# Last 128 tokens of the second product stored in column pieces, on two queues

## The chip, the core and the metric

The kernel runs on one core of a Trainium2 chip. The time is that of the whole program on the device, in microseconds (us), as the median of several runs. A profile comes from one further execution; its span runs from the first to the last instruction that the profiler records.

## What is computed

The reference is an attention layer followed by a two-layer perceptron. Shapes: q, k and v are 8 batches x 12 heads x 448 positions x 64; w_in is 768 x 2048, w_out 2048 x 768; the output has 3584 tokens (8 x 448) of 768 float32 values.

```
scores = scale * np.matmul(q, k.transpose(0, 1, 3, 2))
attn = softmax(scores)
x = np.matmul(attn, v)  ->  (B * S, H * D)
h = x @ w_in
g = np.maximum(0.01 * h, h)
return (g @ w_out).astype(np.float32)
```

## The kernel before, in words

**Attention.** The work goes by units `u` of one batch and two heads (48 of them). `load` brings q, k and v, `cast` turns them to bfloat16 on GpSimd, `scores` and `expo` make the exponentials on TensorE and ScalarE, `pv` multiplies by v (L214) and VectorE divides by the sum (L221, L222). The result is turned into `xT`, with the channels on the partitions.

**The perceptron.** `mlp(i)` takes the tokens in eight blocks, one for each batch, with limits `cuts` that are multiples of 128: seven blocks begin at or a little before the batch's start, and the last has 512 tokens, 3072 to 3583. First, 16 groups of six matmuls (L265) with w_in give `h`, through ScalarE's leaky rectifier (L269). Then `todo` lists, for each 128 tokens `c`, two halves `w` of the 768 output columns (NW = 384). Each entry is a group of 16 matmuls (L283) of 384 columns into one PSUM tile; VectorE copies it into its half of the SBUF tile `o[c]` (L287); after the second half `store` writes the 128 rows to DRAM. PSUM tiles of these groups come from a pool of two buffers (`ps_g`), `o` tiles from a pool of three.

**The store.** Token rows in DRAM aren't in the order in which they lie in `o`: position j of a batch is row 4 * (j % 112) + j // 112. So 128 tokens fall into two row ranges, each of which is one DMA with a stride, and `store` issues both on SP's queue (L247), one after the other. For the last 128 tokens (3456 to 3583) the ranges are 16 and 112 rows, of 48 KB and 336 KB.

**Order.** The program writes the order of every engine's instructions by hand (`manual_schedule`). The generator `mlp(i)` yields after each group, and between groups clusters of the next batch's attention are placed. The last block has none left: its 16 groups with w_in and eight groups with w_out follow one another on TensorE, and nothing but its own copies and stores lies beside them. ScalarE's queue has one DMA in the whole program, a load at the start.

Of the kernel before, what the change touches and what calls it, by code (L numbers as in the profile page):

```python
# [16 lines left out]
def kernel(  # L17
# [9 lines left out]
    nc = tc.nc  # L27

    B, H, S, D = q.shape
    DM, DF = moe_w_in.shape  # L30
    P = 128
# [4 lines left out]
    MD = DF // P  # L36
    NW = DM // 2
# [3 lines left out]
    cuts = [((b * S) // P) * P for b in range(B)] + [B * S]  # L41
# [39 lines left out]
    w_out_sb = w_pool.tile([P, MD, DM], BF16)  # L81
# [154 lines left out]
        nc.vector.tensor_copy(dst, tr[:, 0, :])  # L236


    def store(o, t0):

        done = 0
        while done < P:
            b, j = divmod(t0 + done, S)
            so, p = divmod(j, SC)
            n = min(SC - p, P - done)
            dst = out[b * S:(b + 1) * S].rearrange("(p so) n -> so p n", so=NSC)
            nc.sync.dma_start(out=dst[so, p:p + n], in_=o[done:done + n, :])  # L247
            done += n


# [2 lines left out]
    def settle():  # L253
        while late:
            expo(*late.pop(0))

    def mlp(i):

        n = cuts[i + 1] - cuts[i]
        at = cuts[i] % NX  # L260
        h = h_pool.tile([P, MD, 4 * P], BF16, name="h")
        for m in range(MD):
            ps = ps_g.tile([P, 4 * P], F32, name="mm", tag="g")
            for kk in range(KD):
                nc.tensor.matmul(  # L265
                    ps[:, :n], w_in_sb[:, kk, ts(m, P)], xT[:, kk, at:at + n],
                    start=(kk == 0), stop=(kk == KD - 1),
                )
            nc.scalar.activation(h[:, m, :n], ps[:, :n], AX.Prelu, alpha=0.01)  # L269
            settle()  # L270
            yield KD * n

        todo = [(c, w) for c in range(n // P) for w in range(2)]
        if i == 0:
            todo.sort(key=lambda cw: cw[1])
        o = {}
        for c, w in todo:
            settle()
            if c not in o:
                o[c] = o_pool.tile([P, DM], F32, name="o")  # L280
            ps = ps_g.tile([P, 4 * P], F32, name="mm", tag="g")
            for m in range(MD):
                nc.tensor.matmul(  # L283
                    ps[:, :NW], h[:, m, ts(c, P)], w_out_sb[:, m, ts(w, NW)],
                    start=(m == 0), stop=(m == MD - 1),
                )
            nc.vector.tensor_copy(o[c][:, ts(w, NW)], ps[:, :NW])  # L287
            if w == 1:
                store(o.pop(c), cuts[i] + c * P)
            yield MD * NW  # L290


    def first(u):
# [68 lines left out]
    for i in range(B):  # L362
        work = list(range(begin[i], begin[i + 1])) if i + 1 < B else []
        n = cuts[i + 1] - cuts[i]
        total = MD * KD * n + n // P * MD * DM
        used, done, groups = 0, 0, 0

        def catch_up():
            nonlocal done
            while done < len(work) and (  # L370
                groups >= early[done] if i == 0 else used * len(work) >= total * (done + 1)
            ):
                settle()
                cluster(work[done])
                done += 1

        catch_up()
        for step in mlp(i):
            used += step
            groups += 1  # L380
            catch_up()
# [30 lines left out]
```

## Time and profile before

| | |
|---|---|
| median of 5 runs | 420.86 us (420.31 to 422.96) |
| profiled execution, in all | 422.54 us |
| its span | 420.7 us |
| TensorE clock granted, mean | 0.998 |
| TensorE busy | 407.9 us (97%) |
| ScalarE, VectorE, GpSimd busy | 227.8, 101.2, 92.4 us |
| L283, matmuls of the second product | 896, 150.4 us busy |
| L287, copies into o | 56, mean 558 ns |
| stores (L247) | 56, landing 1.7 to 4.8 us after issue |

A line of the profile names the program line, the engine, the operation, the tiles and their shape, and then the busy time and the mean of one. PE is TensorE, PEld its weight loads, DVE is VectorE, ACT ScalarE, SP the engine that issues most DMAs; a q after a name (SPq, ACTq) means the engine's instruction queue, where a DMA's issue shows. Matmuls are pipelined, so one's duration is longer than the step from one to the next. "Landing" is the time from a DMA's issue to its completion count.

### The profile page before, as it was taken

The numbers are of one execution on the slowest core, as the hardware profiler recorded it, in microseconds if no ns is written. First come the engines' busy times: TensorE is split into PE (matmuls) and PEld (weight loads), VectorE is DVE, ScalarE is ACT, GpSimd is POOL, SyncE is SP. The second block draws the span as 40 slices with busy tenths as digits, with TensorE's granted clock in tenths as the row PEclk, the third lists the DMA queues.
The fourth block names the chain that finished last, engine by engine and source line by source line (L and its number), as shares of the span: only waits on it lengthen the run. The fifth ranks groups of instructions, "written<-read, shape, count | busy, mean of one in ns | idle before, by whom it ended". The sixth has DMA issues, their size and how long they took to land.

```text
span 420.7 us, 9026 instructions
## 1 busy us (share of the span) xinstructions
PE 407.9 (97%) x3745; PEld 234.9 (56%) x3745; DVE 101.2 (24%) x274; ACT 227.8 (54%) x322; POOL 92.4 (22%) x169
## 2 busy tenths in 40 slices
PE   7987999999999999999999999999999999999995
PEld 2664666554566656554565656555465666654562
DVE  2551433211132213220122311321032211320021
ACT  4967783377542784467724585467643577214200
POOL 4863334330211312121311112131130200000000
PEclk9999999999999999999999999999999999999999
DMA  9999999973576748585475656758274431130022
GB/s 198 237 245 245 249 249 243 291 197 88 123 175 175 184 101 218 142 203 132 100 170 153 184 141 162 196 152 196 73 169 131 122 53 24 50 88 0 0 76 75
DMA packets 96649, 63.20 MB, mean 150 GB/s; under 512 B 53600, under 2 KB 93024, under 8 KB 96608
## 3 DMA queue, kind: packets, MB, share of 16 engines
q1 hardware_dynamic: 89072, 56.10, 54.2%
q0 software_dynamic: 7296, 6.29, 9.2%
q8 instruction: 29, 0.48, 0.5%
q10 hardware_dynamic: 240, 0.23, 0.2%
q14 instruction: 12, 0.10, 0.1%
HBM read 45.61 MB, written 11.01 MB: 135 GB/s over the span
## 4 chain that ended last, share of the span: by engine, by line
PE 86%; DMA 12%; POOL 1%; DVE 1%; issue 0%; SPq 0%
PE mm L283 35%; PE mm L265 32%; PE pv L214 10%; PE sc L196 8%; DMA fv<-in_v_dram 5%; DMA fk<-in_k_dram 4%; DMA fq<-in_q_dram 2%; DVE o L287 0%; PE tr L181 0%; POOL w_in_sb L123 0%; POOL qkb L109 0%; POOL v L110 0%; DVE x L222 0%; POOL qkb L108 0%; PE tr L235 0%
## 5 line engine op out<-in xcount | busy, mean ns | idle before, releaser
L205 ACT ACTIVATE e<-sc 112x896 bf16<-112x896 f32 x192 | 164.6, 921 | 101.9 <-PE sc L196 101.8
L265 PE MATMUL mm<-xT,w_in_sb 128*128 128x384 bf16 (+1 forms) x768 | 150.7, 352 | 0.2 <-DVE x L222 0.2
L283 PE MATMUL mm<-w_out_sb,h 128*128 128x384 bf16 x896 | 150.4, 326 | 0.5 <-DVE x L222 0.2
L283 PEld LDWEIGHTS <-h 128*128 128x128 bf16 x896 | 85.9, 98 | 55.7 <-issue 0.7
L265 PEld LDWEIGHTS <-w_in_sb 128*128 128x128 bf16 x768 | 72.8, 98 | 66.1 <-issue 1.0
L269 ACT ACTIVATE h<-mm 128x384 bf16<-128x384 f32 (+1 forms) x128 | 69.8, 545 | 61.8 <-PE mm L265 61.8
L110 POOL CAST v<-fv 112x512 bf16<-112x512 f32 x48 | 29.7, 618 | 215.0 <-PE pv L214 196.3
L214 PEld LDWEIGHTS <-e 112*128 112x128 bf16 x1536 | 56.6, 98 | 26.1 <-issue 16.4
L214 PE MATMUL pv<-v,e 112*128 112x65 bf16 x1536 | 65.7, 194 | 0.5 <-ACT e L205 0.5
L287 DVE COPY o<-mm 128x384 f32<-128x384 f32 x56 | 31.2, 558 | 134.0 <-PE mm L283 134.0
L221 DVE RECIPROCAL rec<-pv 112x4 f32<-112x4 f32 x96 | 17.5, 182 | 151.6 <-PE pv L214 151.3
L196 PE MATMUL sc<-qkT 64*128 64x448 bf16 x384 | 49.1, 353 | 1.1 <-DVE qkT L185 0.7
L222 DVE TENSOR_TENSOR x<-pv,rec 112x256 bf16<-112x256 f32 x96 | 40.7, 424 | 3.3
L108 POOL CAST qkb<-fq 112x512 bf16<-112x512 f32 x47 | 29.0, 618 | 12.0 <-DMA fq<-in_q_dram 10.3
L109 POOL CAST qkb<-fk 112x512 bf16<-112x512 f32 x47 | 29.0, 617 | 10.6 <-DMA fk<-in_k_dram 10.5
L196 PEld LDWEIGHTS <-qkT 64*128 64x128 bf16 x384 | 13.7, 94 | 19.0 <-issue 9.7
L185 DVE COPY qkT<-tr 128x896 bf16<-128x896 bf16 (+1 forms) x15 | 8.8, 589 | 18.2 <-PE tr L181 18.2
L181 PE MATMUL tr<-ident,qkb 112*128 112x112 bf16 x112 | 8.7, 218 | 3.0 <-POOL qkb L109 2.2
L181 PEld LDWEIGHTS <-qkb 112*128 112x128 bf16 x112 | 6.7, 99 | 5.9 <-POOL qkb L109 2.7
L135 PE MATMUL mm<-warm 128*128 128x512 bf16 x13 | 5.1, 552 | 1.2 <-DVE warm L130 1.2
L235 PE MATMUL tr<-ident,x 112*128 112x112 bf16 x36 | 3.3, 215 | 1.3 <-DVE x L222 1.1
L236 DVE COPY xT<-tr 128x448 bf16<-128x448 bf16 x9 | 3.5, 392 | 3.4 <-PE tr L235 3.4
(18 smaller groups left out, 14.7 us busy)
## 6 DMA issues: line engine op xcount, KB each, us to landing
fq<-in_q_dram SPq DMA_DIRECT2D x48, 224.0 KB, 3.7
fv<-in_v_dram SPq DMA_DIRECT2D x48, 224.0 KB, 4.1
fk<-in_k_dram SPq DMA_DIRECT2D x47, 224.0 KB, 3.9
w_in_sb<-in_moe_w_in_dram POOLq DMA_DIRECT2D x4, 768.0 KB, 19.5
w_out_sb<-in_moe_w_out_dram POOLq DMA_DIRECT2D x4, 768.0 KB, 35.3
out_dram<-o SPq DMA_DIRECT2D x8, 336.0 KB, 3.2
out_dram<-o SPq DMA_DIRECT2D x8, 288.0 KB, 2.6
out_dram<-o SPq DMA_DIRECT2D x8, 240.0 KB, 3.9
```

What stands on the lines that cost most here:

```text
L108: by[0](qk_sb[u][:, 0].rearrange("p so h d -> p h so d"), fq)
L109: by[1](qk_sb[u][:, 1].rearrange("p so h d -> p h so d"), fk)
L110: by[2](v_sb[u % NV][:, :, :, :D], fv)
L196: nc.tensor.matmul(ps[:, j, :S], t[j * D:(j + 1) * D, S + c * SC:S + c * SC + P], t[j * D:(j + 1) * D, :S], start=True, stop=True,)
L205: nc.scalar.activation(e[:, :, c, :], sc_t.pop((u, c))[:SC, :, :S], AX.Exp, scale=scale)
L214: nc.tensor.matmul(ps[:, qc, :], e[:, at:at + P], vt[:, j, c, :], start=(c == 0), stop=(c == NSC - 1),)
L221: nc.vector.reciprocal(rec, ps[:SC, :, D:])
L222: nc.vector.tensor_mul(x_t[u][:, :, j, :], ps[:SC, :, :D], rec.to_broadcast([SC, NSC, D]))
L265: nc.tensor.matmul(ps[:, :n], w_in_sb[:, kk, ts(m, P)], xT[:, kk, at:at + n], start=(kk == 0), stop=(kk == KD - 1),)
L269: nc.scalar.activation(h[:, m, :n], ps[:, :n], AX.Prelu, alpha=0.01)
L283: nc.tensor.matmul(ps[:, :NW], h[:, m, ts(c, P)], w_out_sb[:, m, ts(w, NW)], start=(m == 0), stop=(m == MD - 1),)
L287: nc.vector.tensor_copy(o[c][:, ts(w, NW)], ps[:, :NW])
```

## The change

It concerns the last 128 tokens of the last block only. Their second half of 384 columns is made in two groups of 192 columns, each with its own 16 matmuls, PSUM tile and copy. After each of the three copies (384, 192 and 192 columns) these columns are stored at once, the 16-row range from ScalarE's queue and the 112-row range from SP's. All other tokens are stored as before, from SP, both ranges with all 768 columns.

```diff
-    def store(o, t0):
+    def store(o, t0, cols=slice(0, DM), queues=(nc.sync, nc.sync)):
 
+        queues = list(queues)
         done = 0
         while done < P:
...
-            nc.sync.dma_start(out=dst[so, p:p + n], in_=o[done:done + n, :])
+            queues.pop(0).dma_start(out=dst[so, p:p + n, cols], in_=o[done:done + n, cols])
             done += n
...
-        todo = [(c, w) for c in range(n // P) for w in range(2)]
+        halves = [slice(0, NW), slice(NW, DM)]
+        todo = [(c, w) for c in range(n // P) for w in halves]
         if i == 0:
-            todo.sort(key=lambda cw: cw[1])
+            todo.sort(key=lambda cw: cw[1].start)
+        if i == B - 1:
+
+            todo[-1:] = [(c, slice(w, w + NW // 2)) for c, w in ((n // P - 1, NW), (n // P - 1, NW + NW // 2))]
...
+            nw = w.stop - w.start
             for m in range(MD):
                 nc.tensor.matmul(
-                    ps[:, :NW], h[:, m, ts(c, P)], w_out_sb[:, m, ts(w, NW)],
+                    ps[:, :nw], h[:, m, ts(c, P)], w_out_sb[:, m, w],
                     start=(m == 0), stop=(m == MD - 1),
                 )
-            nc.vector.tensor_copy(o[c][:, ts(w, NW)], ps[:, :NW])
-            if w == 1:
-                store(o.pop(c), cuts[i] + c * P)
-            yield MD * NW
+            nc.vector.tensor_copy(o[c][:, w], ps[:, :nw])
+            t0 = cuts[i] + c * P
+            if i == B - 1 and c == n // P - 1:
+                store(o[c], t0, w, (nc.scalar, nc.sync))
+            elif w.stop == DM:
+                store(o.pop(c), t0)
+            yield MD * nw
```

## The prediction

> **What bounds the kernel now.** I read the page's chain first, then the same chain for the last 30 us, then the timeline, the stores' own rows and the stretches after the last matmul. The page's chain gives where the span goes:
>
> ```profile
> ## 4 chain that ended last, share of the span: by engine, by line
> PE 86%; DMA 12%; POOL 1%; DVE 1%; issue 0%; SPq 0%
> ```
>
> TensorE sets the pace, and what this change touches of it is only the end. The chain from 390 us on (start us, us, what):
>
> ```profile
> 389.84 4.96 PE mm L265 x23
> 394.81 20.81 PE mm L283 x128
> 415.62 0.02 issue
> 415.64 0.56 DVE o L287
> ```
>
> The 128 matmuls of the last block's second product run with no gap, 20.81/128 = 162.6 ns each, and stop at 415.62. The span ends at 420.7. So about 5.1 us lie after the last matmul, with TensorE idle, and all of the change's possible gain is in them. The timeline from 415 us shows their start:
>
> ```profile
> 415.64 0.56 DVE L287 COPY o<-mm 128x384 f32<-128x384 f32 x1 [2.04 <-PE mm L283]
> 416.23 0.78 SPq L247 DMA_DIRECT2D out_dram<-o  x2
> ```
>
> The rows of the two stores there (min/median/max of the issue in ns, first and last start), and SP's waits from 395 us:
>
> ```profile
> L247 SPq DMA_DIRECT2D out_dram<-o x2: 314/364/413, 416.2 to 416.6; - x2
> DMA to landing us min/median/max: 1.7/2.3/2.8
> ...
> SPq L407 <- DMA out_dram<-o: 2.3, 1, 2.3
> ```
>
> SP issues the 16-row store at 416.23 and the 112-row one at about 416.6. The larger lands last, 2.8 us after its issue, at 419.4: SP begins its final wait at 417.1 and waits 2.3 us, which agrees. The last 1.3 us to 420.7 are the program's closing waits and barrier (L407). The stretches show the bytes (the last two columns are the DMA share and GB/s):
>
> ```profile
> 416.50:417.00 0.50, 0.00 (x0) 0.00 (x0) 0.00 (x0) 0.00 (x0) 0.00 (x0) 1.00 0.00 0
> 417.00:417.50 0.50, 0.00 (x0) 0.00 (x0) 0.00 (x0) 0.00 (x0) 0.00 (x0) 1.00 0.52 98
> 417.50:418.00 0.50, 0.00 (x0) 0.00 (x0) 0.00 (x0) 0.00 (x0) 0.00 (x0) 1.00 1.01 277
> 418.00:418.50 0.50, 0.00 (x0) 0.00 (x0) 0.00 (x0) 0.00 (x0) 0.00 (x0) 1.00 0.94 295
> 418.50:419.00 0.50, 0.00 (x0) 0.00 (x0) 0.00 (x0) 0.00 (x0) 0.00 (x0) 1.00 0.30 117
> 419.00:419.50 0.50, 0.00 (x0) 0.00 (x0) 0.00 (x0) 0.00 (x0) 0.00 (x0) 0.70 0.00 0
> ```
>
> Nothing moves until 417.0, some 0.8 us after the first issue; 384 KB then move in 2 us; the landing follows the last byte by 0.4 to 0.5 us. So the end is 0.56 copy, 0.4 of a second issue queued behind a first, 0.8 before bytes move, up to 2 moving, 0.4 landing, 1.3 closing.
>
> **What the skill says.** The Trainium skill, "TensorE: Matmul & The Clock Gate", Back-to-back issue gap, gives N/2.4 + 2.5 ns for a full-clock matmul of N columns: 162.5 ns at 384, which the trace has (162.6). The same section says that a stream with a weight load for each matmul keeps about 81 ns at N = 128; here the trace is faster, as shown below, and decides. "VectorE: DVE Perf Modes", The TRN2 errata, has a PSUM copy at (120 + FD) cycles of 0.96 GHz, 525 ns at 384 columns; the trace has 558. "DMA: Bandwidth & Descriptors", Anatomy of one DMA, has a fixed cost of about 2.0 us that doesn't shrink with size, for transfers from GpSimd's path; here SP's 48 KB store lands in 1.7, so the fixed part is no more than that. Issuing engines are not separate DMA queues, on the same page, says that a second issuing engine saves only the issue time: here that is the 0.4 us between 416.2 and 416.6.
>
> **The change part by part**, for the last 128 tokens alone. Up to 413.0 nothing else differs: the engines' instruction streams are the same before that point.
>
> Matmuls. The last group of 16 by 384 columns (162.6 ns, 2.60 us) becomes 32 by 192, with 16 more weight loads. At 192/2.4 + 2.5 = 82.5 ns they take 2.64 us: +0.04. Is a weight load every 82.5 ns affordable? The attention's product loads weights for each 65 columns:
>
> ```profile
> 201.13 0.68 PE L214 MATMUL pv<-v,e 112*128 112x65 bf16 x16
> 201.66 0.38 PE L265 MATMUL mm<-xT,w_in_sb 128*128 128x512 bf16 x1
> ```
>
> Sixteen start within 201.66 - 201.13 = 0.53 us, 33 ns each, loads included. So loads don't bind at 82.5; I take +0.04, bounds 0 and +0.3. The extra group takes a third turn of the two PSUM buffers: its second piece starts at 413.02 + 1.32 = 414.34 and needs the buffer that the copy of 413.05 frees at 413.61. Cover 0.7 us, cost nothing; without it, the rest of one 0.56 copy.
>
> Copies. The 384-column copy becomes two of 192. Against the float32 reads of PSUM in L222 (256 columns, 424 ns) L287 (384, 558) gives (558 - 424)/128 = 1.05 ns a column, so 192 columns take 558 - 201 = 357 ns. The first (414.37 to 414.73) lies beside the second piece's matmuls. The last ends at 415.66 + 0.02 + 0.36 = 416.04 instead of 416.20: -0.16 with the matmuls' +0.04 in it. The copies into the other columns don't wait for the earlier column stores; they wait for TensorE only.
>
> Issues. Two stores become six. SP: 112 rows by 384 columns at about 413.64, 112 by 192 at 414.76, 112 by 192 at 416.07, each about 0.41; ACT: the 16-row halves at the same moments, about 0.43 each (its one DMA issue in this trace, at 0.74 us, took 428 ns). Nothing is queued behind on either: ACT's last Prelu ends at 395.4, SP has only the closing waits. The waits on the eighth DMA before (the shared counts) fall on stores issued by 406.2, landed at 409. The first four stores lie beside matmuls; if they didn't, each would add its 0.4. The last 112-row store is now first on its queue: its issue goes from 416.61 to 416.07, -0.54 in all (0.16 copy, 0.38 queue).
>
> Landing. The last store is 84 KB on SP and 12 KB on ACT, in place of 336 and 48. The 0.8 before bytes and 0.45 after them stay: 1.25. The moving part: 96 KB at the 277 to 295 GB/s of the stretches is 0.35; rows of 768 B in place of 3072 B may halve that rate: 0.7. So 1.6 to 1.95 by this sum; stores of 96 KB elsewhere in the kernel land in a median of 2.1, beside other traffic. I take 1.9, bounds 1.5 and 2.4. Against 2.8: -0.9. The previous column store was issued 1.3 us earlier and has moved its bytes by then. ACT's part is 1/8 of the bytes and should land with SP's or before. Its queue rests from the start on; an extra of 0 (its first load landed in 4.4, SP's beside it in 4.1 to 6.4) to 0.6 (the one long drain of ACT's queue, 627 ns) for it is possible; I take 0. The closing 1.3 stay.
>
> Sum: 416.07 + 1.9 + 1.3 = 419.3 against 420.7, so -1.4 (0.16 + 0.38 + 0.9). The profiled execution took 422.54 in all, 1.84 outside its span; it would take 421.1. The profiled execution stands 1.68 above the median of the five (420.31 to 422.96); taken off the median, 420.86 - 1.4 = 419.4, -0.34%.
>
> **The rivals.**
> (a) The stores shrink but their landing hardly does, from 768-byte rows or ACT's part landing late: 2.4 to 2.6 in place of 1.9. For: 48 KB stores elsewhere have a median of 2.7. Against: the final pair's own 48 KB took 1.7 with nothing else moving. Gain 0.7 to 0.9: 420.1.
> (b) The change does nothing that is seen: the closing waits, with ACT's counts and its end in them, take back what the landing gives. For: the closing 1.3 are not broken down. Against: SP's wait on the stores, 2.3 us, is the last real wait. Only the copy's share remains: 420.7.
> (c) More than forecast: bytes start at 0.7 and the small store's moving part vanishes, landing 1.2: -2.1, 418.7. That is the floor of this mechanism.
> (d) Slower: weight loads bind the 192-column matmuls in the last group. By the skill's load price ("TensorE: Matmul & The Clock Gate", LDWEIGHTS: 128/1.2 = 107 ns) wholly uncovered, a pair takes 107 + 80 = 187 ns, an estimate: 32 of them 6.0 us, +3.4 in place of +0.04, so 2.0 slower: 422.9. It decides from (2.60 + 1.47)/32 = 127 ns a pair. Against it: 162.6 ns at 384 with a load each, and 33 ns at 65 columns.
>
> **How the numbers follow.** Forecast 0.62, (a) 0.18, (b) 0.08, (c) 0.08, (d) 0.04. A measurement of this kernel can tell about 0.5%, 2.1 us, from no change; the forecast lies inside that. Faster by more takes (c), or the forecast with a favourable landing and the runs' scatter (their span is 2.65 us), about a quarter of its 0.62: 0.24. Slower by more is mostly (d): 0.04. Within: 0.72. The range takes the forecast with its landing bounds (1.5 to 2.4: 419.0 to 419.9), (a) and (b) whole and most of (c), with some of the scatter: 418.5 to 421.0.
>
> **What would show it.** Right: 32 matmuls at 82 to 83 ns apart; a last copy near 0.36 us; SP's last store issued 0.4 us after the last matmul's end; ACT's beside it; a landing of 1.6 to 2.1 and SP's final wait near 1.5; 1.3 us from landing to end; no difference before 413. Wrong: a pair of load and matmul above 127 ns, a store of ACT landing after SP's by over 0.5, a landing still near 2.6, a closing part above 1.3, or a span that differs before the last group.

## The result and the profile after

| | before | after |
|---|---|---|
| median | 421.86 us (419.4 to 424.91, 80 runs) | 420.34 us (417.49 to 423.24, 43 runs) |
| profiled execution, in all / span | 422.54 / 420.7 us | 421.02 / 419.2 us |
| last matmul's end to the span's end ("tail") | 5.12 us | 3.52 us |

The ratio is 0.9967 with a 95% interval of 0.9953 to 0.9980: 0.33% or 1.4 us faster (0.84 to 1.98 us, from the interval times 421.86). The interval leaves out 1, so the gain is real, but it is below the 0.5% that the prediction named as the least that can be told from no change.

A single span cannot tell 1.4 us apart here, since runs of one kernel differ by 5 us. The tail can: it is read within one execution, as the span less the end of the last matmul. The profile's page prints spans and landings to 0.1, which leaves a tail good to about 0.05; the trace itself keeps both to a nanosecond (the spans are 420.737 and 419.240 us). Where a tail, a landing or a closing part has two decimals below, it is read from the trace.

The chain from 390 us on, of the kernel after (start us, us, what):

```profile
389.91 4.96 PE mm L266 x23
394.87 20.85 PE mm L289 x144
415.72 0.02 issue
```

144 matmuls stand in place of 128 and take 20.85 us in place of 20.81; the copy behind them takes 0.36 in place of 0.56 (next lines). The 0.06 by which the second product starts later comes from ahead of it. The timeline of the end:

```profile
415.75 0.36 DVE L293 COPY o<-mm 128x192 f32<-128x192 f32 x1 [0.96 <-PE mm L289]
416.13 0.32 SPq L248 DMA_DIRECT2D out_dram<-o  x1
416.14 0.38 ACTq L248 DMA_DIRECT2D out_dram<-o  x1
```

The 112-row store is issued 0.41 us after the last matmul's end (416.13 - 415.72); before, it was about 1.0. The landings of the stores of the last two pieces, from the issues by size, and SP's waits for them at the end (in all, times, longest):

```profile
out_dram<-o SPq DMA_DIRECT2D x2, 84.0 KB, 1.8
out_dram<-o ACTq DMA_DIRECT2D x2, 12.0 KB, 1.9
```

```profile
SPq L416 <- DMA out_dram<-o: 1.4, 2, 1.2
```

The last stores land 1.8 and 1.9 us after their issues where the larger one took 2.8, and the wait shrinks from 2.3 to 1.4. The bytes (last two columns: DMA share, GB/s):

```profile
416.80:417.00 0.20, 0.00 (x0) 0.00 (x0) 0.00 (x0) 0.00 (x0) 0.00 (x0) 1.00 0.12 31
417.00:417.20 0.20, 0.00 (x0) 0.00 (x0) 0.00 (x0) 0.00 (x0) 0.00 (x0) 1.00 0.82 215
417.20:417.40 0.20, 0.00 (x0) 0.00 (x0) 0.00 (x0) 0.00 (x0) 0.00 (x0) 1.00 0.72 212
417.40:417.60 0.20, 0.00 (x0) 0.00 (x0) 0.00 (x0) 0.00 (x0) 0.00 (x0) 1.00 0.13 35
```

Again some 0.8 us pass from issue to bytes; then about half a microsecond of moving, in place of 2; then the last landing at 418.09 and 1.15 us of closing part to 419.24. Before, the last landing was at 419.39 and the closing part took 1.35 us. The rows of SP's closing waits from the last landing on, before and after:

```profile
L407 SPq EVENT_SEMAPHORE  x8: 28/28/28, 419.4 to 419.8; - x8
L416 SPq EVENT_SEMAPHORE  x5: 28/28/28, 418.1 to 418.3; - x5
```

SP waits for eight completion counts of DMAs, one after another in a fixed order, and the DMAs from SP and ACT use these counts in turn. A wait whose count is already there still takes about 0.06 us until the next. Before, the store that lands last was on the first of the eight counts, so all eight waits were still to run; with six stores in place of two it is on the fourth, and five are left. In the 14 profiles of this case the closing part follows the number of waits left: 1.35 us with eight, 1.28 with seven, 1.21 with six, 1.15 or 1.16 with five, 1.09 to 1.11 with four, 1.03 or 1.04 with three, 0.97 with two (with five pieces counted from the landing that SP was waiting for). So 0.20 of the tail's 1.60 us came from the number of stores and not from their bytes.

The two profiles hold no other difference that I can lay to the change: up to 395 us TensorE is busy 387.24 us before and 386.99 after.

### The profile page after: what moved, and what is told of

The parts are those of the page before. It is cut to its first block, busy times and chain, and to the rows that moved or that the text cites. A ratio compares the mean times of both kernels' runs of the same rounds, so it can differ in the third digit from the quotient of the medians.

```text
span 419.2 us, 9068 instructions
## 1 busy us (share of the span) xinstructions
PE 407.7 (97%) x3761; PEld 236.2 (56%) x3761; DVE 101.3 (24%) x275; ACT 227.8 (54%) x322; POOL 92.4 (22%) x169
## 4 chain that ended last, share of the span: by engine, by line
PE 86%; DMA 12%; POOL 1%; DVE 1%; issue 0%; SPq 0%
PE mm L289 35%; PE mm L266 32%; PE pv L214 11%; PE sc L196 8%; DMA fv<-in_v_dram 5%; DMA fk<-in_k_dram 4%; DMA fq<-in_q_dram 2%; DVE o L293 0%; PE tr L181 0%; POOL w_in_sb L123 0%; POOL qkb L109 0%; POOL v L110 0%; DVE x L222 0%; POOL qkb L108 0%; PE tr L235 0%
## 5 line engine op out<-in xcount | busy, mean ns | idle before, releaser
L289 PE MATMUL mm<-w_out_sb,h 128*128 128x384 bf16 (+1 forms) x912 | 150.2, 323 | 0.5 <-DVE x L222 0.2
L289 PEld LDWEIGHTS <-h 128*128 128x128 bf16 x912 | 87.0, 98 | 54.6 <-issue 0.5
L293 DVE COPY o<-mm 128x384 f32<-128x384 f32 (+1 forms) x57 | 31.4, 551 | 133.5 <-PE mm L289 133.5
```

Source lines behind the costliest of these rows:

```text
L289: nc.tensor.matmul(ps[:, :nw], h[:, m, ts(c, P)], w_out_sb[:, m, w], start=(m == 0), stop=(m == MD - 1),)
L293: nc.vector.tensor_copy(o[c][:, w], ps[:, :nw])
```

## The experiments

Theory: the tail is a sum of the last copy, the issues, a landing that depends on the bytes still to move, and a closing part taken as constant; nothing ahead of it matters. The rivals were that one part (the second queue, or the mere cut) makes the gain, that landing is all fixed cost, or that the tail isn't on what the time measures. All edits are against the changed kernel unless said otherwise. Ratios are to the kernel before, with 95% intervals. These intervals are about as wide as the effects and mostly overlap, so what each part is worth is read from the tails.

**Queues alone.** The second half stays one group of 384 columns, and all 768 columns are stored once, on the two queues.

```diff
-            todo[-1:] = [(c, slice(w, w + NW // 2)) for c, w in ...]
+            pass
...
-            if i == B - 1 and c == n // P - 1:
-                store(o[c], t0, w, (nc.scalar, nc.sync))
-            elif w.stop == DM:
-                store(o.pop(c), t0)
+            last = i == B - 1 and c == n // P - 1
+            if w.stop == DM:
+                store(o.pop(c), t0, queues=(nc.scalar, nc.sync) if last else (nc.sync, nc.sync))
```

> The tail is the time from the last matmul's end to the span's end: 5.1 us before, 3.5 us after. Here only the queue part of the change is made: the last 128 tokens keep two groups of 384 columns and one store of all 768 columns, with the 16 rows on ACT's queue and the 112 rows on SP's. Theory of the sum (copy, queued issue, landing by bytes, constant closing part): only the queued issue of about 0.35 goes, tail 0.02 + 0.56 + 0.03 + 2.8 + 1.25 = 4.7 us, time 0.1% shorter, not to be told from no change. Rival, a second queue is worth nothing since the transfers share the same engines: tail 5.1 us. Rival, the second queue makes most of the gain: tail at or under 4.0 us.

Measured: tail 421.6 - 416.70 = 4.9 us, ratio 0.9999 (0.9976 to 1.0021). The rows of its two last stores:

```profile
L248 SPq DMA_DIRECT2D out_dram<-o x1: 316/316/316, 417.3 to 417.3; - x1
L248 ACTq DMA_DIRECT2D out_dram<-o x1: 380/380/380, 417.3 to 417.3; - x1
...
DMA to landing us min/median/max: 2.7/2.8/2.9
```

Both are issued at once, so the prediction's 0.38 (0.37 by the trace) is gone from the issue; but only 0.24 is gone from the tail (5.12 to 4.88), between the theory and the first rival. The small store, alone ahead of the large one before (1.7 us), now lands at 2.7 beside it, and the large one takes 2.92 in place of 2.79. A reading that fits, but was not tested: before, the small store's 48 KB moved while the large one was not yet moving, so part of the delay was put to use. At the 277 to 295 GB/s of the stretches before, 48 KB take 0.17 us, an estimate, and 0.37 - 0.17 = 0.20.

**Two halves.** Columns cut once, no short group.

```diff
-            todo[-1:] = [(c, slice(w, w + NW // 2)) for c, w in ...]
+            pass
```

> The last 128 tokens in two groups of 384 columns as before, but each half stored at once, 16 rows from ACT and 112 from SP; no group of 192. Theory of the sum: copy 0.56, landing of the 168 KB store 2.3 us as the first piece's in the changed kernel, so tail 0.02 + 0.56 + 0.03 + 2.3 + 1.25 = 4.2 us. Rival, a landing that hardly depends on size once the columns are cut (rows of 768 and 1536 bytes cost alike): tail near 3.7 us. Rival, it's the short last group that matters and the halves bring no more than the queue: tail 4.7 us.

Measured: tail 419.0 - 414.78 = 4.2 us, ratio 0.9965 (0.9944 to 0.9986); the last stores' row:

```profile
DMA to landing us min/median/max: 2.2/2.3/2.4
```

The theory's 4.2 came out, and both rivals (3.7 and 4.7) fall. Half the bytes take 0.5 off the landing (2.9 to 2.4).

**Short copy alone.** Groups and copies of 384, 192, 192, but the last two pieces stored together.

```diff
-                store(o[c], t0, w, (nc.scalar, nc.sync))
+                if w.stop != 576:
+                    store(o[c], t0, slice(w.start // NW * NW, w.stop), (nc.scalar, nc.sync))
```

> Groups and copies of 384, 192 and 192 columns as in the changed kernel, but the two last pieces stored together: 384 columns and 384 columns, both ranges on ACT and SP. Against the run with two halves it changes the last copy alone. Theory of the sum: the last copy 0.36 in place of 0.56, landing 2.3 us, tail 0.02 + 0.36 + 0.03 + 2.3 + 1.25 = 4.0 us. Rival, a copy's end does not set the issue: 4.2 us as with two halves.

Measured: tail 417.6 - 413.65 = 4.0 us, ratio 0.9966 (0.9945 to 0.9987). Against the two halves only the last groups and copies changed. The tail is 0.28 us shorter (3.97 against 4.25): 0.20 is the copy, which is thus on the path as expected, and 0.07 is one closing wait less.

**All pieces on SP.**

```diff
-                store(o[c], t0, w, (nc.scalar, nc.sync))
+                store(o[c], t0, w)
```

> All three column pieces as in the changed kernel, but both row ranges on SP's queue, 16 rows first. Theory of the sum: the last 112-row store is issued 0.35 us later, behind the 16-row one, tail 3.5 + 0.35 = 3.85 us; the issues of the earlier pieces lie beside matmuls and cost nothing. Rival, ACT's store lands last in the changed kernel and sets its end, so its queue costs as much as it saves: tail 3.5 to 3.6 us.

Measured: tail 419.1 - 415.39 = 3.7 us, ratio 0.9960 (0.9936 to 0.9984). Between the two again: the second queue is worth 0.17 us (3.69 against 3.52), not 0.35. The rival has its share in that: in the changed kernel the 84 KB store lands 2.20 us after the last matmul, 0.39 earlier than the 2.59 here, but ACT's 12 KB store lands 0.17 behind it and sets the end, and one closing wait more is left. The rows of the last two stores:

```profile
L248 SPq DMA_DIRECT2D out_dram<-o x2: 314/362/411, 415.8 to 416.2; - x2
...
DMA to landing us min/median/max: 1.4/1.6/1.8
```

**SP alone, larger range first.** `store` collects its ranges and issues the 112 rows ahead of the 16, for the last 128 tokens.

```diff
-    def store(o, t0, cols=slice(0, DM), queues=(nc.sync, nc.sync)):
+    def store(o, t0, cols=slice(0, DM), queues=(nc.sync, nc.sync), big_first=False):
...
-        done = 0
+        done, todo = 0, []
...
-            queues.pop(0).dma_start(out=dst[so, p:p + n, cols], in_=o[done:done + n, cols])
+            todo.append((n, dst[so, p:p + n, cols], o[done:done + n, cols]))
             done += n
+        if big_first:
+            todo.sort(key=lambda r: -r[0])
+        for n, dst, src in todo:
+            queues.pop(0).dma_start(out=dst, in_=src)
...
-                store(o[c], t0, w, (nc.scalar, nc.sync))
+                store(o[c], t0, w, big_first=True)
```

> All column pieces on SP's queue as in the run without ACT (tail 3.7 us, the 16-row store landing 1.4 and the 112-row store 1.8 after their issues, 0.4 apart), but the 112-row range issued first. Theory: the order decides what the second issue costs. The larger lands 1.8 after the first issue, the smaller 0.4 + 1.4 = 1.8 after it, so tail 0.02 + 0.36 + 0.03 + 1.8 + 1.25 = 3.5 us, as with two queues. Rival, the second issue always costs its 0.2 to 0.4: tail 3.7 us.

Measured: tail 414.9 - 411.48 = 3.4 us, ratio 0.9959 (0.9940 to 0.9979). One queue does as well as two when the larger range is issued first. The 16 rows are then the last to land, 0.2 us behind the 112 (their issue is 0.37 later, their landing 0.15 shorter), so the second issue costs 0.2 and no longer its whole length.

```profile
L253 SPq DMA_DIRECT2D out_dram<-o x2: 317/367/417, 411.9 to 412.3; - x2
...
DMA to landing us min/median/max: 1.6/1.6/1.7
```

**Queues exchanged.**

```diff
-                store(o[c], t0, w, (nc.scalar, nc.sync))
+                store(o[c], t0, w, (nc.sync, nc.scalar))
```

> The changed kernel with the two queues exchanged: 16 rows on SP, 112 rows on ACT. ACT's issue took 0.38 us in the changed kernel and SP's 0.32. Theory of the sum with equal queues: tail 3.5 to 3.6 us. Rival, a store from ACT lands later than one of its size from SP: the larger range then sets the end, tail 3.7 us or more.

Measured: tail 418.9 - 415.50 = 3.4 us, ratio 0.9967 (0.9945 to 0.9989). The landings of the last two pieces by size:

```profile
out_dram<-o ACTq DMA_DIRECT2D x2, 84.0 KB, 1.8
out_dram<-o SPq DMA_DIRECT2D x2, 12.0 KB, 1.5
```

ACT's 112-row store lands in 1.8 us as SP's did, so a large store is not slower from ACT; the 16 rows take 1.5 from SP and took 1.9 from ACT. The last landing is now 2.22 us after the last matmul, 0.37 earlier than on SP alone: here the second queue saves the whole second issue.

**All at the end.** The kernel before, with the last block's stores issued behind its last copy, the last chunk's first.

```diff
-    o_pool = ctx.enter_context(tc.tile_pool(name="o", bufs=3))
+    o_pool = ctx.enter_context(tc.tile_pool(name="o", bufs=4))
...
-            if w == 1:
+            if w == 1 and i < B - 1:
                 store(o.pop(c), cuts[i] + c * P)
             yield MD * NW
+        for c in reversed(list(o)):
+            store(o.pop(c), cuts[i] + c * P)
```

> The kernel before, with the stores of the last block's four 128-token chunks all put behind the last chunk's on SP's queue, so that 1536 KB instead of 384 KB move after the last matmul (a fourth buffer for o). Theory, the tail's moving part is bytes by rate and on the path one for one: 1152 KB more at some 280 GB/s are 4.2 us, tail 9.3 us and time 4 us longer (1.0%). Rival, the tail is fixed costs and bytes are cheap: the eight issues at 0.4 set it, tail 7.5 us or less. Rival, the tail is not on what the time measures: no change of time.

Measured: tail 424.6 - 415.01 = 9.6 us, ratio 1.0107 (1.0069 to 1.0144, from six runs), 4.5 us slower (2.9 to 6.1). Here the effect is far above the scatter: a tail 4.5 us longer is a time 4.5 us longer. Its eight issues are done by 420.1, while bytes still move at 323 GB/s at 421.7 and thin out by 422.4, so the bytes and not the issues set this end:

```profile
415.62 4.50 SPq L247 DMA_DIRECT2D out_dram<-o  x8
```

```profile
421.64:421.84 0.20, 0.00 (x0) 0.00 (x0) 0.00 (x0) 0.00 (x0) 0.00 (x0) 0.50 0.87 323
...
422.24:422.44 0.20, 0.00 (x0) 0.00 (x0) 0.00 (x0) 0.00 (x0) 0.00 (x0) 0.50 0.17 62
```

**Four pieces.** 384, 192, 96, 96.

```diff
-            todo[-1:] = [(c, slice(w, w + NW // 2)) for c, w in ...]
+            todo[-1:] = [(n // P - 1, slice(a, z)) for a, z in ((NW, 576), (576, 672), (672, DM))]
```

> The last 128 tokens in column pieces of 384, 192, 96 and 96, each stored at once as in the changed kernel. Tail 3.5 us in the changed kernel. Theory of the sum: the last copy has 96 columns, 558 - 288 x 1.05 = 256 ns, 0.10 less; the last 112-row store has 42 KB in place of 84, at 250 GB/s 0.17 us less; tail 3.2 us. Rival, rows of 384 bytes move no faster than rows of 768 and the landing's fixed part is reached: only the copy's 0.10 goes, tail 3.4 us. Rival, the 96-column matmuls are held up by their weight loads: groups of 16 take over 0.68 us and the last matmul ends later.

Measured: tail 415.4 - 412.42 = 3.0 us, ratio 0.9950 (0.9932 to 0.9968). The gain is larger than the theory's sum (3.2), and the rivals fall: the landing is 1.6 at most, and the product takes 20.89 us, 0.04 more than with three pieces. What the sum lacked is a landing 0.30 shorter in place of 0.17 (1.95 to 1.65), and two closing waits fewer, 0.12 us.

```profile
391.53 20.89 PE mm L289 x160
412.42 0.02 issue
412.45 0.26 DVE o L293
```

```profile
DMA to landing us min/median/max: 1.5/1.6/1.6
```

**The changed kernel again**, unaltered.

> The changed kernel once more, unaltered, for a second profile of its end and for a comparison with finer pieces on the same chip. If the end is fixed by its steps, tail 3.5 us within 0.1, though the span may differ by 2 us from other places. If the tail itself scatters by several tenths, the attribution by tails falls.

Measured: tail 418.6 - 415.04 = 3.6 us, ratio 0.9979 (0.9959 to 0.9999). Read from the trace it is 3.52 us, as in the first profile, though the last matmul ends 0.7 us earlier.

**Four pieces on SP**, larger range first: the edits of "Four pieces" and of "SP alone, larger range first" together.

> Pieces of 384, 192, 96 and 96 columns, all on SP's queue, 112 rows first. Tail 3.0 us with these pieces on two queues, 3.4 with pieces of 192 on SP alone. A 96-column group takes 0.69 us and SP's two issues 0.32 + 0.42 = 0.74, so SP falls behind by about 0.05 a piece. Theory, the second queue saves only issue time and there is just enough of it: tail 3.0 to 3.1 us. Rival, ACT's queue is what makes the short pieces pay: tail 3.3 us or more.

Measured: tail 418.1 - 414.43 = 3.7 us, ratio 0.9963 (0.9939 to 0.9988). The rival holds and my theory fell. The rows of the last stores show why:

```profile
L253 SPq DMA_DIRECT2D out_dram<-o x4: 370/396/418, 414.4 to 415.7; - x4
```

When the last copy begins (414.45), SP has just begun the issue of the previous piece's 112 rows, and three more follow, each 0.37 to 0.42 us. An issue behind another costs about 0.4, not 0.32, and two of them exceed the 0.69 us that a 96-column group takes. With short pieces SP's issuing is the bound, and there the second queue pays: 3.7 against 3.0.

**Five pieces.** 384, 192, 96, 48, 48, on two queues.

```diff
-            todo[-1:] = [(c, slice(w, w + NW // 2)) for c, w in ...]
+            todo[-1:] = [(n // P - 1, slice(a, z)) for a, z in ((NW, 576), (576, 672), (672, 720), (720, DM))]
```

> Pieces of 384, 192, 96, 48 and 48 columns on ACT and SP. Theory of the sum: the last copy 558 - 336 x 1.05 = 206 ns, 0.05 less than with four pieces; landing 1.5 against 1.6; tail 2.8 to 2.9 us, less what the 48-column matmuls cost if their weight loads bind (33 ns each at 65 columns, 22 by columns alone: 0.3 us on the last matmul's end, which the tail doesn't show but the second product's length does). Rival, rows of 192 bytes move as slowly as rows of 384, so landing stays at 1.6 or grows: tail 3.0 us or more.

Measured: tail 419.2 - 416.07 = 3.1 us, ratio 0.9959 (0.9938 to 0.9980). No better than four (3.10 against 3.00), which is the rival's number, but not for the rival's reason: the landing does shrink (1.57 against 1.65), and the last store lands 1.92 us after the last matmul in place of 1.96. The closing waits take it back. With ten stores the eight counts are used up and begin again: SP's last store is on the first count, and when it lands (417.8) eight waits are left, where the four pieces have three.

```profile
L416 SPq EVENT_SEMAPHORE  x8: 28/28/28, 417.8 to 418.3; - x8
```

The product takes longer too:

```profile
394.95 21.12 PE mm L289 x176
416.07 0.02 issue
416.10 0.21 DVE o L293
```

It takes 21.12 against 20.89 us, where each of the two splits before had added 0.04, so the 48-column matmuls are held to more than their columns. With the tail, five pieces lose some 0.3 us against four.

**Four pieces, queues exchanged**, for a second profile of the pieces with the shortest tail: the edits of "Four pieces" and of "Queues exchanged" together.

> Pieces of 384, 192, 96 and 96 columns with 16 rows on SP and 112 on ACT, a second profile of the best pieces. With the first arrangement of the queues the tail was 3.0 us and the ratio to the kernel before 0.995; exchanging them took 0.1 from the tail with 192-column pieces. Theory of the sum: tail 2.9 to 3.0 us, ratio 0.995 within its interval. Rival, the 3.0 was a lucky execution: tail 3.2 us or more.

Measured: tail 420.8 - 417.87 = 2.9 us, ratio 0.9954 (0.9933 to 0.9974). So the 3.0 was no luck. The tail of four pieces is 0.5 shorter than that of three with either arrangement of the queues (3.52 to 3.00 and 3.38 to 2.90); in time their intervals overlap with those of three pieces, so that four are the better version is shown by the tails and only suggested by the ratios.

## Why the prediction was right

- **Matmuls.** +0.04 was forecast and +0.04 measured (20.85 against 20.81). Rival (d), with a load and a matmul of 192 columns at 127 ns or more, is out.
- **Last copy.** 357 ns was forecast, and the two took 357 and 358. The run with the short copy alone shows it on the path.
- **Issue.** The 112-row store goes out 0.41 us after the last matmul's end, as forecast (416.07 - 415.66). The issues themselves are shorter than taken, 0.32 on SP and 0.38 on ACT in place of 0.41 and 0.43; nothing depends on it here.
- **Landing.** 1.9 us was taken; it is 1.79 on SP and 1.95 on ACT. The bytes move at 212 to 215 GB/s in the fullest stretches, between the 277 to 295 of before and the half of it that was allowed for. So rival (a) with 2.4 is out, and (c) with 1.2 too.
- **Closing part.** 1.3 us was taken as constant. It went from 1.35 to 1.15, so (b), in which it grows, is out; but it is not constant.
- **Sum.** -1.4 us was forecast; the tail has -1.60 in both profiles of the changed kernel, less the 0.04 of the product, and the ratio -1.4 (-0.84 to -1.98).

The number by itself says less. The forecast of 419.4 was 0.9 below the measured 420.34, because it was taken off the median of five runs, 420.86, and the median of 80 is 421.86. Rival (a)'s 420.1 lies nearer to the measured median; only the landing and the tail tell the two apart.

In order of time the 1.60 us are about 0.20 of copy, 0.37 of issue, 0.84 of landing and 0.20 of closing part. The forecast had 0.20, 0.38, 0.9 and nothing (its 0.16 is the copy's 0.20 less 0.04 of matmuls). Two terms are mis-sized.

"The closing 1.3 stay" is the first. Rival (b) said that this part was not broken down, and only asked whether it grows. Three of its eight waits were over when the last store landed, and 0.20 us went with them.

The second is the 0.38 of the queue. It is in the issue times, but a second queue alone shortens the tail by 0.24 (before to queues alone), and the changed kernel's is 0.17 shorter than that of SP alone. In the first case the large store then takes 0.13 longer to land; in the second ACT's small store lands last and sets the end. Built up by runs, the parts are: queues 0.24 (5.12 to 4.88), halves stored at once 0.63 (to 4.25), the short copy 0.28 (to 3.97), its own store 0.45 (to 3.52). So the two cuts of the stores bring 1.08, of which 0.12 are two closing waits. That the total came out so near is partly luck: what the forecast gave too much to the queue it gave too little to the stores and to the closing part.

I also expected ACT's part to land with SP's or before. It lands 0.17 later, although it has an eighth of the bytes. With the queues exchanged the 16 rows land first, in 1.5 us. The queue alone does not decide the order: with the same arrangement ACT's store lands last in "Two halves" (2.36 against 2.19) and SP's in "Short copy alone" (2.35 against 2.18). Why stays open.

## What to carry to other kernels

At the end of a kernel, price what follows the last matmul as a sum: last copy, issue, the wait until bytes move, bytes by rate, receipt, closing waits. The copy, the bytes and the issues can be cut, and the closing waits depend on which count the last store is on (0.97 to 1.35 us here), so that more stores can shorten or lengthen them. Cut the last output by columns so that the last piece is small, and issue the larger store first; here a second queue was needed only when the pieces came faster than one queue issued them (96 columns, 3.7 against 3.0 us). Where runs scatter by more than the effect, measure the stretch itself inside each profile, and check with one exaggerated run that the stretch is on the time.

## What the runs showed that I had not expected

The scatter of the profiled executions comes from the start of the program, not from its end. In three of the profiles the last matmul ends at 411.5, 415.6 and 417.9 us. The first weight load of the second block's L265 is at 80.0, 84.2 and 86.4 us, so from there on all three take the same time, 331.4 to 331.5 us. TensorE's busy time in the first 60 us goes the same way. The larger-range-first run:

```profile
0.00:60.00 60.00, 55.47 (x700) 34.47 (x701) 24.88 (x69) 47.68 (x66) 31.77 (x66) 1.00 1.14 253
```

the kernel before:

```profile
0.00:60.00 60.00, 52.75 (x645) 31.75 (x646) 23.39 (x64) 44.14 (x60) 30.64 (x64) 1.00 1.13 237
```

and four pieces with the queues exchanged:

```profile
0.00:60.00 60.00, 51.74 (x615) 30.62 (x617) 21.81 (x59) 42.55 (x58) 30.27 (x63) 0.97 1.13 236
```

The DMA engines have work in all of this stretch, and the GB/s in the last column are 253, 237 and 236. Between the first two it may be that the loads came faster; this was read from the profiles and not tried. Between the last two the rates agree, but the granted clock of TensorE (the column before the DMA share) is 0.97 in place of 1.00. At most that accounts for 3% of 60 us, 1.8 us, an estimate, of the 2.2 us between them. So two causes, loads and clock, have a part that these runs do not separate, and either can be worth as much as the whole change.
